# Key products 6 and 7 of the first parity in the opening, high copies ahead of low parts, and attention as a pipeline over units

## The chip, the cores and the metric

One core of a Trainium2 chip. The metric is the device time of one execution in microseconds, the median over several runs. Five engines work side by side, each from its own queue in order: TensorE (PE, matrix products), VectorE (DVE), ScalarE (ACT), GpSimd (POOL) and SyncE (SP). In this kernel POOL and SP mostly issue DMAs; a DMA that adds to what lies at its target (an accumulating DMA) is issued by POOL.

## The reference

The kernel mixes two branches of one input x (2048 tokens, 512 channels, fp32) by a gate per token. Branch a is local dilated attention (32 heads of 16, each token sees 8 tokens at distances 0, 2, ..., 14), branch b a gated feed-forward layer of width 1792:

```python
qkv = (x @ wqkv)                    # q, k, v for 32 heads of 16
idx = pos[:, None] - arange(8) * 2
logits = einsum("bhsd,bhswd->bhsw", q, k[idx]) * 16 ** -0.5    # masked where idx < 0
a = einsum("bhsw,bhswd->bhsd", softmax(logits), v[idx]) @ wo
b = (gelu(x @ w_gate) * (x @ w_up)) @ w_down
g = sigmoid((x * gate_w).sum(-1))
out = g * a + (1 - g) * b
```

## The kernel before

Tokens are handled in two parities (`par` 0 and 1, even and odd tokens), since the dilation of 2 never mixes them. Within a parity, tokens lie in 128 partitions of 8 each.

**Products in two halves.** Every fp32 operand is split in a high part (a copy rounded to fp32r) and a low part (the operand minus that copy), and a product is three matmuls: high by high, low by high, high by low. So each operand costs a ScalarE copy and one more step, in one of two ways: `split` (L82) copies on ScalarE and subtracts on VectorE; `split_by_dma` (L219) writes the negative on ScalarE, lets an accumulating DMA on POOL's queue add the operand, and copies the high part on ScalarE. Both forms stand all over the kernel: in `hidden` (L743) for the hidden activations, in `down_w` (L709) for the weights of the down product, in `operands` (L660) for gate and up.

**Seven products for eight.** Products of 2x2 blocks are made from seven block products with sums of operands (`s1` to `s4` of x, `t1` to `t4` of the weights), in the keys and queries (list `KEYS`, L450), the values (`values`, L335) and gate and up (`gate_up`). `sum_x` and `combine_b` make the sums on VectorE. `XOP` holds the split x operands, `QO` the split weights of the keys, `VO` those of the values.

**Stages.** An opening (from L1053) loads x and weights and does five of the seven key products of parity 0 by hand (`key_mm`, `third`), with part of the values. `values` then does the rest of the values and `ffn(0)` the feed-forward layer of parity 0 in 14 chunks of 128 hidden units (f = 0 to 13). In each chunk `gate_up` places seven gate and up products, with four `pieces` between them: in chunks f = 0 and 1 these are key products 6 and 7 (`key_one`, L467; indices 5 and 6 of `KEYS`), later they are down products (`down`) of the group of two chunks before. Then `keys` and `values` do parity 1's first products (the crossing between the parities), and `ffn(1)` its chunks. `key_one` also copies its bank to a tile `rt` on ScalarE (L473) and issues two accumulating DMAs on POOL's queue, into the stores of keys and queries in HBM (`store_b`, L462).

**Attention.** A generator `attention` (L589) runs over eight units (2 parities x 4 groups of 128 channels). For each unit `load_kq` loads keys and queries from the stores, `scores` multiplies and reduces on VectorE (L512, L515), `softmax` (L523) does maximum, subtraction, an exp on ScalarE, sum, reciprocal and scaling, and `mix` (L541) multiplies with the values and adds up (L552 to L560), then transposes and stores. All this is VectorE work but for the exp. `softmax` also issues a tiny exp on a tile `ahead` (L527), which brings the exp table into ScalarE ahead of the real exp (L531).

**What sets the order.** The program is written once in order, and a scheduler puts the instructions of each engine in a queue by priorities. Attention steps are drawn by `pull(budget)` between products: each yield of the generator names its cost, and `PACE` scales the budgets for parity 0 and 1. They get a priority 150 places behind their place (`BEHIND`). `paced` ties a step to the matmul before it, and `PIN` keeps the opening's VectorE steps in program order. The tiles rotate through few buffers (`BUFS`): `hh` and `hl` have six each and serve both as hidden activations and as stage tiles of the opening and the values (`stages`), `rt` has four. A generator `first` (L1166), drawn between the value products, makes the operands of chunk 0 and the sums t1 and b22 that key products 6 and 7 need.

## Time and profile before

| | |
|---|---|
| median of 3 runs | 606.97 us (605.94 to 610.77) |
| profiled execution | 604.98 us |
| its span, first to last instruction | 603.2 us |
| mean granted TensorE clock | 0.999 |
| instructions | 8342 |
| DMA | 144.07 MB, mean 239 GB/s |
| chain that ended last, share by engine | PE 42%, DVE 4%, DMA 3%, ACT 3% |

Busy times are shares of the span: an engine at 98% has 2% of idle time in all, and what it waited for in that time is what could be won. Each instruction's duration overlaps with its neighbour's, so a rate is read from starts, not from durations. A wait is named by the instruction that waited and the one that released it: "PE p L347 <- ACT s L354" is a matmul of line 347 into a bank p that stood until a ScalarE step of line 354 wrote or freed s.

### The profile page before, as it was taken

How to read it: one execution, taken by the hardware profiler on the slowest of the kernel's cores; microseconds unless marked ns; L12 is line 12 of the kernel's file. 1: busy time of each engine (PE TensorE's matmuls, PEld its weight loads, DVE VectorE, ACT ScalarE, POOL GpSimd, SP SyncE). 2: the span in 40 equal slices, each digit the busy share in tenths (PEclk: the TensorE clock that was granted, in tenths of full speed). 3: DMA queues.
4: the chain of work that ended last, by engine and by line, in shares of the span. 5: the costliest groups of instructions: out<-in, count | busy, mean ns of one | idle time of the engine just before them, and what ended most of it. 6: DMA issues, size and time to landing. Idle time of an engine off the chain costs nothing.

```text
span 603.2 us, 8342 instructions
## 1 busy us (share of the span) xinstructions
PE 589.9 (98%) x2743; PEld 488.5 (81%) x2743; DVE 529.5 (88%) x613; ACT 438.6 (73%) x777; POOL 131.2 (22%) x153
## 2 busy tenths in 40 slices
PE   9999999999999999999999999999999999999997
PEld 7779877788888887787889888888888888887885
DVE  6776998999899996999998998999799979896981
ACT  6669566678887769877877666667876877697732
POOL 0131572212121202112101382212121213131400
PEclk9999999999999999999999999999999999999999
DMA  8689999997898888899889999989979797976924
GB/s 305 204 237 293 274 275 284 245 271 203 237 254 217 246 242 225 228 265 322 262 257 310 271 287 271 273 209 250 283 166 265 179 277 173 277 163 203 124 68 156
DMA packets 98152, 144.07 MB, mean 239 GB/s; under 512 B 9023, under 2 KB 59327, under 8 KB 98110
## 3 DMA queue, kind: packets, MB, share of 16 engines
q1 hardware_dynamic: 74862, 105.08, 52.9%
q0 software_dynamic: 22960, 38.09, 35.8%
q8 instruction: 21, 0.34, 0.2%
q10 hardware_dynamic: 288, 0.39, 0.2%
q14 instruction: 21, 0.17, 0.1%
HBM read 69.83 MB, written 44.66 MB: 190 GB/s over the span
## 4 chain that ended last, share of the span: by engine, by line
PE 42%; DVE 4%; DMA 3%; ACT 3%; issue 1%; SPq 0%; POOL 0%; DVEq 0%; ACTq 0%
PE p L728 18%; PE p L775 6%; PE acc L775 6%; PE p L1000 5%; PE acc L459 2%; PE acc L1000 2%; DMA hl<-c 1%; PE acc L347 1%; PE p L347 1%; DMA g<-vwt 1%; DVE prod L512 1%; DVE S L87 1%; DVE g L234 1%; DVE raw L244 0%; DMA raw<-os 0%
## 5 line engine op out<-in xcount | busy, mean ns | idle before, releaser
L728 PE MATMUL p<-S,g 128*128 128x512 f32 x672 | 168.4, 389 | 0.6 <-ACT p L810 0.6
L728 PEld LDWEIGHTS p<-S,g 128*128 128x128 f32 x672 | 125.9, 188 | 27.0 <-ACT p L810 1.1
L728 PE MATMUL p<-A,g 128*128 128x512 f32 x504 | 126.6, 390 | 0.0
L728 PEld LDWEIGHTS p<-A,g 128*128 128x128 f32 x504 | 94.2, 188 | 20.2 <-DMA g<-raw 0.4
L512 DVE TENSOR_TENSOR prod<-kq 128x2048 f32<-128x2048 f32 x32 | 72.9, 2279 | 5.8 <-DMA kq<-kq 5.4
L552 DVE TENSOR_TENSOR prod<-v,lg 128x2048 f32<-128x2048 f32 x32 | 73.0, 2280 | 1.0
L515 DVE TENSOR_REDUCE lg<-prod 128x128 f32<-128x2048 f32 x32 | 73.0, 2280 | 0.1
L775 PE MATMUL p<-d,hh 128*128 128x512 f32 x224 | 69.0, 392 | 2.3 <-ACT p L769 1.6
L686 POOL DMA_DIRECT2D g<-raw x28 | 24.2, 866 | 180.2 <-ACT g L683 84.1
L775 PE MATMUL acc<-d,hh 128*128 128x512 f32 x224 | 59.6, 391 | 2.0 <-DMA d<-r 1.3
L739 ACT ACTIVATE c<-p 128x512 f32<-128x512 f32 x56 | 33.4, 597 | 31.7 <-PE p L728 24.0
L775 PEld LDWEIGHTS p<-d,hh 128*128 128x128 f32 x224 | 41.7, 188 | 12.7 <-ACT p L769 3.1
L775 PEld LDWEIGHTS acc<-d,hh 128*128 128x128 f32 x224 | 41.9, 188 | 11.7 <-DMA d<-r 1.7
L744 DVE TENSOR_TENSOR c<-c 128x512 f32<-128x512 f32 x56 | 37.9, 680 | 7.6 <-ACT c L841 7.5
L740 DVE TENSOR_TENSOR c<-c,s 128x512 f32<-128x512 f32 x56 | 38.0, 685 | 6.4 <-ACT c L739 6.4
L775 PE MATMUL p<-d,hl 128*128 128x512 f32 x112 | 42.6, 389 | 0.0
L733 ACT ACTIVATE s<-p 128x512 f32<-128x512 f32 x56 | 33.1, 592 | 10.6 <-PE p L728 10.0
L751 POOL DMA_DIRECT2D hl<-c x24 | 22.9, 971 | 75.6 <-ACT hl L750 49.6
L556 DVE TENSOR_TENSOR prod<-prod 128x1024 f32<-128x1024 f32 x32 | 39.0, 1220 | 0.4
L719 POOL DMA_DIRECT2D d<-r x23 | 19.7, 858 | 90.0 <-ACT d L718 47.1
L459 PE MATMUL acc<-d,S 128*128 128x512 f32 x144 | 35.7, 390 | 0.0
L775 PE MATMUL acc<-d,hl 128*128 128x512 f32 x112 | 35.2, 391 | 0.3 <-DVE hl L748 0.2
(209 smaller groups left out, 1076.4 us busy)
## 6 DMA issues: line engine op xcount, KB each, us to landing
g<-raw POOLq DMA_DIRECT2D x28, 512.0 KB, 6.3
raw<-wff SPq DMA_DIRECT2D x42, 256.0 KB, 4.6
ws<-g SPq DMA_DIRECT2D x14, 768.0 KB, 6.0
g<-ws SPq DMA_DIRECT2D x14, 768.0 KB, 6.8
r<-wff SPq DMA_DIRECT2D x28, 256.0 KB, 4.3
hl<-c POOLq DMA_DIRECT2D x24, 256.0 KB, 6.6
d<-r POOLq DMA_DIRECT2D x23, 256.0 KB, 6.9
v<-vs SPq DMA_DIRECT2D x8, 512.0 KB, 7.0
```

The lines of the kernel that those rows point to most:

```text
L459: LAST[:] = [nc.tensor.matmul(ps, x[:, ts], w, start=(start and kc == i == 0), stop=(kc == 1 and i == 2), skip_group_check=True)]
L512: paced(nc.vector.tensor_tensor(prod, spans(k, jj), q[:, jj:jj + 2, None, :].to_broadcast([P, 2, W, UC]), op=OP.mult))
L515: nc.vector.tensor_reduce(two_of(lg, jj), prod.rearrange("p j w (h d) -> p (j w) h d", d=DH), axis=AX.X, op=OP.add)
L552: paced(nc.vector.tensor_tensor(prod.rearrange("p j w (h d) -> p (j w) h d", d=DH), spans(v, jj).rearrange("p j w (h d) -> p j w h d", d=D ...
L556: nc.vector.tensor_tensor(prod[:, :, :4], prod[:, :, :4], prod[:, :, 4:], op=OP.add)
L728: LAST[:] = [nc.tensor.matmul(ps, w_, a_, start=(start and kc == 0 and n == 0), stop=(kc == 1 and n == 2), skip_group_check=True)]
L733: nc.scalar.activation(s, ps, AF.Copy)
L739: nc.scalar.activation(c, ps, AF.Copy)
L740: nc.vector.tensor_tensor(c, c, s, op=OP.add)
L744: nc.vector.tensor_tensor(ge, ge, up, op=OP.mult)
L775: LAST[:] = [nc.tensor.matmul(pp, a[:, ts], w, start=(i == 0 and n == 0 and gr == 0), stop=(i == 1 and n == 2), skip_group_check=True)]
L1000: LAST[:] = [nc.tensor.matmul(pa, a, b, start=(first and n == 0), stop=(last and n == 2), skip_group_check=True)]
```

## The change

- The opening takes key products 6 and 7 of parity 0: after `third(4)` it calls `key_one(0, k, t)` for k = 5 and 6 and all four t. Chunks f = 0 and 1 of `ffn(0)` have empty pieces. In parity 0 `key_one` writes its copies into stage tiles (`hh` and `hl` in turn) instead of `rt`. The sums t1 and b22 are made in the opening, no longer in `first`.
- In the opening the high copies are issued in one go on ScalarE (`late_split`, `late_s`, `late_b`), and the low parts wait in a list `low` from which `lows(n)` issues n at a time on VectorE.
- `hidden` uses the form with the VectorE subtract for all chunks; before, chunks with even f above 0 used the accumulating DMA. `down_w` uses it for f < 3 in both parities (before: f < 2 and f < 3).
- Attention: `softmax` is cut into `exps` (up to the exp) and `shares` (from the sum), and the `ahead` step is dropped. Scores and exps of the next unit come before the mix of this one, its shares after. Values are loaded ahead of that (`load_values`), and the keys of the unit after next ahead of the mix.
- `PACE` goes from (1.05, 1.22) to (1.1, 1.25).

```diff
-PACE = (1.05, 1.22)
+PACE = (1.1, 1.25)
...
-        st = tl("rt")
+        st = tl("rt" if par else next(stages))[:, :512]
...
-    def softmax(par, u):
+    def exps(par, u):
         lg = LG[par, u]
         m = pool.tile([P, UH, NP], F32, name="m")
         nc.vector.tensor_reduce(m, lg, axis=AX.X, op=OP.max)
-        nc.scalar.activation(pool.tile([P, 32], F32, name="ahead")[:W, :1], m[:W, 0, :1], AF.Exp, scale=0.0)
         yield 0.7
         nc.vector.tensor_tensor(lg, lg, m[:, :, :, None].to_broadcast([P, UH, NP, W]), op=OP.subtract)
         yield 0.7
         nc.scalar.activation(lg, lg, AF.Exp, scale=DH ** -0.5)
+
+    def shares(par, u):
+        lg = LG[par, u]
+        m = pool.tile([P, UH, NP], F32, name="m")
         nc.vector.tensor_reduce(m, lg, axis=AX.X, op=OP.add)
...
+        def logits(i, wait):
+            if units[i] not in LG:
+                load_kq(*units[i])
+                if wait:
+                    yield LOAD
+            yield from scores(*units[i])
+            yield from exps(*units[i])
+            ready.append(i)
...
         for i, un in enumerate(units):
-            if scored == i:
+            if i not in ready:
                 yield from need(un[0], un[1] // 2 * 2)
-                load_kq(*un)
-                yield LOAD
-                yield from scores(*un)
-                scored += 1
-                mixed = False
-            yield from need(un[0], 1)
-            yield from softmax(*un)
...
+                yield from logits(i, i > 0)
+            if i not in shared:
+                yield from share(i)
+            load_values(*un)
+            if keyed(i + 1):
+                yield from logits(i + 1, False)
+                if keyed(i + 2):
+                    load_kq(*units[i + 2])
+            yield from mix(*un)
             done.add((*un, "o"))
...
+            if i + 1 in ready:
+                yield from share(i + 1)
...
     def down_w(par, f):
...
-        if f < 2 + par:
+        if f < 3:
...
     def hidden(key, ge, up):
...
-        if key[0] % 2 or not key[0]:
-            nc.scalar.activation(hh_, ge, AF.Copy)
-            nc.vector.tensor_tensor(hl_, ge, hh_.bitcast(F32), op=OP.subtract)
-        else:
-            nc.scalar.activation(hl_, ge, AF.Copy, scale=-1.0)
-            nc.gpsimd.dma_start(hl_.bitcast(F32), ge, accum_op=OP.add)
-            nc.scalar.activation(hh_, ge, AF.Copy)
+        nc.scalar.activation(hh_, ge, AF.Copy)
+        nc.vector.tensor_tensor(hl_, ge, hh_.bitcast(F32), op=OP.subtract)
...
-                pieces = [[lambda t=t: key_one(par, 5 + f, t)] for t in range(BT)]
+                pieces = [[lambda t=t: key_one(par, 5 + f, t)] if par else [] for t in range(BT)]
...
+    def late_split(name, kc, x):
+        hi, lo, raw = x
+        nc.scalar.activation(hi, raw, AF.Copy)
+        low.append((lo, raw, hi))
+
+    def lows(n):
+        for _ in range(n):
+            lo, raw, hi = low.pop(0)
+            paced(nc.vector.tensor_tensor(lo, raw, hi.bitcast(F32), op=OP.subtract))
...
     third(2)
     room_b("t4")
+    lows(1)
     for kc in range(2):
         combine_b("t4", "b21", "b21", "t2", kc)
-        split_b("t4", kc)
-        split_x(0, 1, 2 + kc)
+        late_b("t4", kc)
+        lows(1)
...
+    room_b("t1")
+    for kc in range(2):
+        combine_b("t1", "b11", "b22", "t2", kc)
+        late_b("t1", kc)
+        lows(2)
     third(3)
+    lows(len(low))
+    room_b("b22")
+    for kc in range(2):
+        late_b("b22", kc)
...
     third(4)
     PIN[0] = False
     done.add((0, 0))
     PACING[0] = True
+    for k in 5, 6:
+        for t in range(BT):
+            key_one(0, k, t)
+            next(made, None)
...
         combine(1)
         fetch_d(0)
-        yield
-        for n in "t1", "b22":
-            room_b(n)
-            for kc in range(2):
-                if n == "t1":
-                    combine_b("t1", "b11", "b22", "t2", kc)
-                split_b(n, kc)
-                yield
```

More of the change, by code (lines that the diff above doesn't have):

```diff
@@ L539, in softmax, with load_values, mix @@
         yield 0.7
-    def mix(par, u, pause):
-        lg = LG.pop((par, u))
+    VT = {}
+    def load_values(par, u):
         hh, c = divmod(u, 2)
-        v = pool.tile([P, 2 * NP - 1, UC], F32, name="v")
+        VT[par, u] = v = pool.tile([P, 2 * NP - 1, UC], F32, name="v")
         load_slots(v, VS[par, hh][c])
-        yield pause
+    def mix(par, u):
+        lg, v = LG.pop((par, u)), VT.pop((par, u))
         tb = pool.tile([P, 2, BT * UC], F32, name="tb")
@@ L590, in attention, with keyed, share @@
         units = [(0, u) for u in range(NU)] + [(1, u) for u in range(NU)]
-        yield from need(0, 0)
-        load_kq(0, 0)
-        yield from scores(0, 0)
-        yield from need(0, 1)
-        scored, mixed = 1, False
+        ready, shared = [], []
+        def keyed(i):
+            return i < len(units) and (units[i][0], units[i][1] // 2 * 2) in done
+        def logits(i, wait):
[6 more added lines that the diff above has]
+            ready.append(i)
+        def share(i):
+            yield from need(units[i][0], 1)
+            yield from shares(*units[i])
+            shared.append(i)
         for i, un in enumerate(units):
-            if scored == i:
+            if i not in ready:
                 yield from need(un[0], un[1] // 2 * 2)
-                load_kq(*un)
-                yield LOAD
-                yield from scores(*un)
-                scored += 1
-                mixed = False
-            yield from need(un[0], 1)
-            yield from softmax(*un)
-            to = units[scored] if scored < len(units) else None
-            ahead = to and (to[0], to[1] // 2 * 2) in done
-            if ahead:
-                load_kq(*to)
-            yield from mix(*un, LOAD if mixed else 0.0)
+                yield from logits(i, i > 0)
[7 more added lines that the diff above has]
+            yield from mix(*un)
             done.add((*un, "o"))
-            mixed = not ahead
-            if ahead:
-                yield from scores(*to)
-                scored += 1
+            if i + 1 in ready:
+                yield from share(i + 1)
     fill = attention()
@@ L1101, in tile_gated_mix, with late_s, late_b @@
               for kc in range(2))
+    low = []
+    def late_split(name, kc, x):
[6 more added lines that the diff above has]
+            paced(nc.vector.tensor_tensor(lo, raw, hi.bitcast(F32), op=OP.subtract))
+    def late_s(n, kc):
+        i = {"s1": 3, "s2": 0, "s4": 1, "s3": 2}[n]
+        raw = S1.pop(kc) if n == "s1" else XR[kc][:, i * 512:(i + 1) * 512]
+        XOP[n, kc] = pair("S")
+        late_split(n, kc, (*XOP[n, kc], raw))
+    def late_b(n, kc):
+        late_split(n, kc, (*QO[n, kc], QR[n, kc]))
     for kc in range(2):
@@ L1104, in tile_gated_mix @@
             sum_x(kc, n)
+        late_s("s2", kc)
         if not kc:
@@ L1109, in tile_gated_mix @@
                 next(made)
-        split_s("s2", kc)
+        else:
+            lows(1)
         combine_b("t3", "b12", "b22", "b12", kc)
         combine_b("t2", "b11", "t3", "b11", kc, OP.add)
-        split_b("t2", kc)
-        if not kc:
-            for t in range(2, BT):
-                take_first(Z_[t], t, first_copy[t % 2])
+        late_b("t2", kc)
+        if kc:
+            lows(2)
+    room_b("t3")
+    for kc in range(2):
+        late_s("s3", kc)
+        late_b("t3", kc)
+        lows(1)
+    for t in range(2, BT):
+        take_first(Z_[t], t, first_copy[t % 2])
     values(0, iter(()), lambda k: None, range(2))
@@ L1122, in tile_gated_mix @@
     PACING[0] = False
-    room_b("t3")
-    for kc in range(2):
-        split_s("s3", kc)
-        split_b("t3", kc)
     def third(k, after=iter(())):
@@ L1143, in tile_gated_mix @@
     room_b("t4")
+    lows(1)
     for kc in range(2):
         combine_b("t4", "b21", "b21", "t2", kc)
-        split_b("t4", kc)
-        split_x(0, 1, 2 + kc)
+        late_b("t4", kc)
+        lows(1)
+    for kc in range(2):
+        late_split("a22", kc, (*X[0, 1, 2 + kc], XR[kc][:, 1536:]))
+        sum_x(kc, "s4")
+        late_s("s4", kc)
     set_x(0)
+    lows(2)
     for kc in range(2):
-        sum_x(kc, "s4")
-        split_s("s1", kc)
-        split_s("s4", kc)
-    third(3)
+        late_s("s1", kc)
+    room_b("t1")
+    for kc in range(2):
+        combine_b("t1", "b11", "b22", "t2", kc)
+        late_b("t1", kc)
+        lows(2)
+    third(3)
+    lows(len(low))
+    room_b("b22")
+    for kc in range(2):
+        late_b("b22", kc)
+    for f in range(2):
+        fetch(f)
     room_v(*LARGE)
@@ L1156, in tile_gated_mix @@
     next(made)
-    for f in range(2):
-        fetch(f)
+    lows(len(low))
     next(made)
@@ L1176, in first @@
         fetch_d(0)
-        yield
-        for n in "t1", "b22":
-            room_b(n)
-            for kc in range(2):
-                if n == "t1":
-                    combine_b("t1", "b11", "b22", "t2", kc)
-                split_b(n, kc)
-                yield
     def step(k):
```

## The prediction

> **What bounds the kernel now.** I read the page's busy times first, then a table of busy time by stage, then what TensorE waited for, then single stretches of the timeline. On the page:

> ```profile
> PE 589.9 (98%) x2743; PEld 488.5 (81%) x2743; DVE 529.5 (88%) x613; ACT 438.6 (73%) x777; POOL 131.2 (22%) x153
> ```

> TensorE is busy for all but 13.3 of the span's 603.2 us. The change neither adds nor drops a matmul (2743 in both instruction orders), so it can win back only a part of those 13.3 us; what it can lose has no such limit. Where they lie is told by the table of stages (length, PE, PEld, DVE, ACT and POOL busy, clock, DMA share, GB/s):

> ```profile
> 0.00:42.00 42.00, 38.75 (x199) 31.26 (x199) 28.92 (x51) 28.30 (x60) 9.70 (x22) 1.00 0.76 246
> 42.00:60.00 18.00, 17.83 (x133) 17.16 (x134) 12.32 (x23) 15.94 (x40) 1.77 (x2) 1.00 0.99 289
> 60.00:84.00 24.00, 24.00 (x107) 19.86 (x107) 23.55 (x24) 12.84 (x27) 14.76 (x12) 1.00 1.15 267
> 84.00:116.00 32.00, 29.18 (x124) 22.55 (x123) 29.75 (x40) 24.37 (x40) 10.45 (x11) 1.00 1.08 281
> 116.00:232.00 116.00, 116.00 (x513) 96.08 (x512) 108.55 (x123) 89.55 (x148) 18.61 (x22) 1.00 0.88 235
> 232.00:246.00 14.00, 12.44 (x52) 9.33 (x52) 10.57 (x11) 13.90 (x22) 2.60 (x3) 1.00 0.86 214
> 246.00:272.00 26.00, 26.00 (x116) 21.52 (x116) 25.90 (x33) 19.96 (x35) 4.28 (x5) 1.00 0.95 264
> 272.00:284.00 12.00, 11.18 (x48) 8.32 (x47) 12.00 (x10) 8.59 (x16) 2.16 (x3) 1.00 1.06 326
> ...
> 520.00:585.00 65.00, 64.69 (x285) 52.99 (x284) 57.53 (x62) 46.99 (x81) 14.61 (x17) 1.00 0.71 155
> 585.00:603.20 18.20, 14.09 (x63) 11.33 (x61) 3.40 (x6) 3.62 (x6) 0.00 (x0) 0.98 0.41 144
> ```

> PE loses 3.25 us in the opening, 2.82 in the first feed-forward chunks (84 to 116), 1.56 at 232 to 246, 0.82 at 272 to 284, 0.31 near the end of the second parity and 4.1 in the tail. The third column shows the other thing to watch: VectorE has 210.3 us of work in the 224 us from 60 to 284, and from 246 to 284 it is full. The waits of PE say who was late:

> ```profile
> PE p L775 <- ACT p L769: 1.6, 3, 0.8
> PE acc L775 <- DMA d<-r: 1.3, 1, 1.3
> PE p L347 <- ACT s L354: 1.3, 1, 1.3
> ...
> PE p L347 <- ACT g L86: 1.0, 1, 1.0
> ...
> PE acc L775 <- ACT rt L473: 0.7, 1, 0.7
> PE p L728 <- ACT p L810: 0.6, 1, 0.6
> ```

> **The opening.** ScalarE's high copies now come ahead of all low parts, and VectorE's subtractions are queued behind them. The two waits of the opening, 1.3 on s (L354) and 1.0 on g (L86), are for ScalarE copies that stood behind a split's turn. I take both as gone: -2.3 us, with bounds of -3.25 (all idle of 0 to 42) and +1.0 (one such wait more). What comes in: 48 matmuls of key products 6 and 7. Their rate is in the timeline of PE, where six take 1.36 us from start to start:

> ```profile
> 105.78 1.52 PE L728 MATMUL p<-A,g 128*128 128x512 f32 x6
> 107.14 0.39 PE L775 MATMUL acc<-d,hl 128*128 128x512 f32 x1
> ...
> 110.43 1.88 PE L775 MATMUL acc<-d,hh 128*128 128x512 f32 x7 [1.31 <-DMA d<-r]
> ```

> So 48 x 0.227 = 10.9 us of PE time moves from the chunks f = 0 and 1 (5.4 each) to the opening: no change in the sum. With them go eight ScalarE copies and, for the sums t1 and b22, six VectorE steps of 0.68 (4.1 us). Both fit: the stage 42 to 60 leaves VectorE 5.7 us idle and becomes 10.9 us longer. Without that room the 4.1 would be late for the first feed-forward chunk.

> The products' 16 accumulating stores move with them on POOL's queue, ahead of the accumulating load of chunk 0's operand g1:

> ```profile
> ks<-rt POOLq DMA_DIRECT2D x8, 128.0 KB, 9.2
> qs<-rt POOLq DMA_DIRECT2D x8, 128.0 KB, 10.1
> ```

> They read the stage tiles hh and hl (before: rt), which the value products want back 10 to 15 us later; with a landing of 9 to 10 us that is just in time. If they landed later, ScalarE would stop at the copy into the tile and all its later copies with it. I take nothing here, and put the price of a late landing into the next part.

> **Chunks f = 0 to 2.** Gone: the wait on rt L473 (0.7), since no key bank is emptied there, and the wait on d<-r (1.3, the row at 110.43), since with f < 3 the chunk's low part comes from a VectorE subtract instead of an accumulating DMA. That is -2.0. On the other side, chunks 0 and 1 have 5.4 us less of PE work each over unchanged ScalarE and VectorE work, and VectorE has 23.55 of 24 us busy at 60 to 84. Nothing before shows a chunk so short; the bounds are 0 and one chunk's lost cover, 5.4 us. Most of the work has its operands made in the longer opening, so I take a value near the lower end, that of a wait which stands there now: +0.8.

> **The hidden halves.** In 24 of 56 halves a ScalarE copy and an accumulating DMA give way to a VectorE subtract:

> ```profile
> L748 DVE TENSOR_TENSOR hl<-c,hh 128x512 fp32r<-128x512 f32 x32 | 21.7, 681 | 4.3 <-ACT hh L747 4.3
> L750 ACT ACTIVATE hl<-c 128x512 fp32r<-128x512 f32 x24 | 15.1, 628 | 4.9 <-DVE c L744 4.9
> L751 POOL DMA_DIRECT2D hl<-c x24 | 22.9, 971 | 75.6 <-ACT hl L750 49.6 <-ACT c L739 10.8 <-DMA os<-tb 9.5
> L512 DVE TENSOR_TENSOR prod<-kq 128x2048 f32<-128x2048 f32 x32 | 72.9, 2279 | 5.8 <-DMA kq<-kq 5.4
> ```

> ScalarE loses 15.1 us and POOL 22.9; VectorE gains 24 x 0.68 = 16.3 (8.2 in each parity). Over the whole kernel that is 546 of 603 us, still under PE. It does no harm where VectorE has slack, and the second parity has it (57.53 of 65 at 520 to 585, so the 0.3 lost there goes too). The first parity is another matter, below.

> **232 to 246.** ScalarE is full there (13.90 of 14), because it swaps tables four times around one `ahead` preload:

> ```profile
> 230.04 1.28 ACT L527 ACT_TABLE_LOAD   x1
> 231.34 0.20 ACT L527 ACTIVATE ahead<-m 8x1 f32<-8x1 f32 x1
> 231.56 1.28 ACT L841 ACT_TABLE_LOAD   x1
> 232.85 0.60 ACT L841 ACTIVATE c<-p 128x512 f32<-128x512 f32 x1
> 233.96 1.28 ACT L531 ACT_TABLE_LOAD   x1
> ...
> 240.63 1.28 ACT L825 ACT_TABLE_LOAD   x1
> ```

> A gelu came between the preload and its exp, so the exp table was loaded twice. Without the preload two loads are left, which frees 2.6 us, and the hidden halves free 0.6 each. I take the waits there as gone, -1.5 of the 1.56. The exp itself now stands behind its own load, but the new order puts a whole mix between exp and its use, so nobody waits. [...]

> **The crossing to the second parity, 272 to 300.** VectorE must split the second parity's sums there. In the changed kernel's order, between the last gelu product of the first parity (it waits for a PE result) and the low part of s2, the first that PE reads across the crossing from a sum, VectorE has 37 steps: 28 of the 128x512 kind, two mix products, two halvings, five small ones. Their spacing:

> ```profile
> 260.18 2.28 DVE L552 TENSOR_TENSOR prod<-v,lg 128x2048 f32<-128x2048 f32 x1
> 262.50 1.23 DVE L556 TENSOR_TENSOR prod<-prod 128x1024 f32<-128x1024 f32 x1
> 263.64 0.68 DVE L744 TENSOR_TENSOR c<-c 128x512 f32<-128x512 f32 x1
> 264.24 0.68 DVE L558 TENSOR_TENSOR prod<-prod 128x512 f32<-128x512 f32 x1
> 264.96 0.42 DVE L560 TENSOR_TENSOR o<-prod 128x256 f32<-128x256 f32 x1
> ```

> 28 x 0.60 + 2 x 2.28 + 2 x 1.2 + 5 x 0.4 = 25.8 us. PE has 85 matmuls between the same points, 85 x 0.227 = 19.3, and the activation that hands the result over takes 0.6 to 0.9. So PE stops for 25.8 + 0.8 - 19.3 = 7.3; I take +7.2. In the order before, about 10 us less of attention stands in that stretch, and the same count gives about 1, as 0.82 was seen. Bounds: +9 if VectorE comes late to the stretch, and 0 if what is queued there overlaps more than these starts show. The old 0.8 goes.

> **The sum.** -2.3 - 2.0 + 0.8 - 1.5 - 0.3 - 0.8 + 7.2 = +1.1 us; the tail keeps its 4.1. The profiled execution took 604.98 us, 1.8 beyond its span; it becomes 606.1. It lies 2.0 under the median of 606.97, with three runs spread over 4.8; on the median's footing it would be 608.1. I predict halfway, 607.0. Its own range is 602 to 612.

> **Rivals.** Faster: the stall at the crossing doesn't come, and the rest of the sum holds: -6.1, or 598.9 to 600.9, say 600; without the 0.8 of chunks 0 and 1, 599. For it: each removed wait stands by name in the list, and at 272 to 284 a full VectorE cost PE only 0.8. Against it: 25.8 us in a room of 19.3. It decides if PE's stall near 290 is under 1.5. Chance 0.2.

> Slower: VectorE bounds the first parity. It has 210.3 us of work from 60 to 284, and gains 8.2 + 0.7 - 4.1 = 4.8, while PE's time there shrinks by 10.9 to 213.1. If VectorE also keeps its 13.7 idle us (waits for ScalarE and DMA), it needs 228.8, 15.7 too much; a start 3.5 earlier (of the 5.4 it waited for kq, L512) leaves 12. The 4.3 of stalls in that stretch (2.0 + 1.5 + 0.8) are swallowed, the opening gives 2.3, and VectorE comes late into the crossing (9 there instead of 7.2, 1.8 more): 12 - 4.3 - 2.3 + 1.8 = +7.2, which is 612.2 by the profiled execution and 614.2 by the median, 613 halfway. It decides once VectorE has no gap before each gelu product from about 120 on. Against it: attention can slide into the second parity. [...] Chance 0.25.

> Late start: the 16 stores in the opening meet DMA engines that are full (share 0.99 at 42 to 60), land late and hold ScalarE: 5.4 instead of 0.8 in chunk 0, +5.7, so 611 to 613. Chance 0.1, half of it beyond 1%.

> The forecast keeps 0.45. One per cent, 6.1 us, is about what can be told from no change here. The faster rival lies beyond it; the slower one stands just beyond 613, and I count 0.2 of its 0.25, with 0.05 of the late start. So 0.2, 0.55, 0.25. The range goes to 599 for the faster rival and 615 for the slower.

> **What would show it.** The PE waits on s L354, g L86, rt L473, d<-r and at 232 to 246 should be gone; ACT_TABLE_LOADs before exp should be single; a PE wait of 5 to 9 us on a VectorE low part (L87, tile S) should stand near 290, with VectorE gapless before it. No such wait, or many waits on hl (L760) at 120 to 260, would make the sum wrong.

## The result, and the profile after

The changed kernel takes 626.98 us in the median (625.34 to 630.68, 4 runs), the kernel before 606.58 (605.94 to 610.77, 4 runs): a ratio of 1.033, with a 95% interval of 1.026 to 1.040. It is slower by some 20 us; I had forecast 607, at most 615. (Further down, the one run of e3_cross and the one of the kernel before that lie over 1.5% above the fastest of their kernel are left out.) The profiled execution took 628.07 us, with a span of 626.3. Its page begins:

```profile
PE 596.8 (95%) x2743; PEld 495.6 (79%) x2743; DVE 539.0 (86%) x638; ACT 423.8 (68%) x743; POOL 109.8 (18%) x128
```

The edits did to the amounts what they say: VectorE gained 9.5 us (the durations of its instructions add up to 17.0 more, as forecast; the page counts time in which two of them overlap once), ScalarE lost 14.8, POOL 21.4, and PE has as many matmuls as before. But PE is idle for 29.5 us instead of 13.3, and it waits for other things than before (PE's waits: us in all, times, longest):

```profile
PE p L783 <- DVE hl L760: 6.6, 1, 6.6
PE acc L459 <- ACT S L128: 6.2, 1, 6.2
PE acc L347 <- DVE c L87: 3.5, 1, 3.5
PE p L741 <- DVE g L692: 2.4, 1, 2.4
PE p L1008 <- DMA S<-raw: 1.7, 1, 1.7
PE p L741 <- ACT c L752: 1.2, 1, 1.2
PE acc L347 <- DMA g<-vwt: 1.1, 1, 1.1
```

None of the waits quoted of before is left, and few long ones have come. To place them I use PE's lateness: the end of a matmul, less the time that all matmuls up to it need at PE's rate at a granted clock of 1.00 (0.2267 us for 512 columns and 0.1183 for 258, whose median spacing in both traces is 0.227 and 0.119; for the 31 warm ones of 128 columns 0.06, an estimate, 128/512 of the 0.2267, where the traces show a spacing of 0.107; 581.1 us in all). It counts a stall and the slow matmuls behind it alike. Worked out from the matmul records of both profiled executions, by stretches of PE's own work, it grows by (us). The wait on d<-r, which the forecast has among the chunks 0 to 2, stands at 98.8 us of work, so its 1.3 is forecast here for the stretch from 98 on:

| PE work done | stretch | before | after | difference | forecast |
|---|---|---|---|---|---|
| 0 to 57 | opening | 7.9 | 5.8 | -2.1 | -2.3 |
| 57 to 98 | end of the values, chunks 0 to 2 | 2.7 | 11.3 | +8.6 | +0.1 |
| 98 to 262 | rest of the first parity | 4.2 | 0.1 | -4.1 | -2.8 |
| 262 to 300 | crossing | 1.5 | 11.6 | +10.1 | +6.4 |
| 300 to 350 | values of the second parity | 0.6 | 1.7 | +1.1 | 0 |
| 350 to 372 | chunk 1 of the second parity | 0.0 | 8.8 | +8.8 | 0 |
| 372 to 581 | rest and tail | 1.2 | 2.1 | +0.9 | -0.3 |

The differences add up to 23.3 us, the difference of the two profiled executions (628.07 - 604.98 = 23.1) but for the tail behind the last matmul. Three stretches lose 27.5 us.

**Chunks 0 to 2.** VectorE's timeline (start, us, engine, instruction, idle time before it and its releaser), with the matmul that waits:

```profile
50.59 0.70 DVE L167 TENSOR_TENSOR v<-v,tb 128x516 f32<-128x516 f32 x1 [0.20 <-PE acc L459]
63.96 2.29 DVE L512 TENSOR_TENSOR prod<-kq 128x2048 f32<-128x2048 f32 x1 [12.67 <-DMA kq<-kq]
66.16 0.69 DVE L87 TENSOR_TENSOR c<-v,c 128x516 fp32r<-128x516 f32 x1
```
```profile
66.91 0.83 PE L347 MATMUL acc<-c,A 128*128 128x258 f32 x4 [3.54 <-DVE c L87]
```

VectorE stands idle for 12.67 us (before: 5.4) for a load that only attention needs. Behind it in VectorE's queue is the low part c, 0.7 us of work whose operands have long been there; PE needs it and stops for 3.54 us. ScalarE stands too, for 4.78 us, until an accumulating store of the key products has read a stage tile:

```profile
65.48 0.38 ACT L354 ACTIVATE hh<-acc 128x256 f32<-128x256 f32 x1 [4.78 <-DMA qs<-hh]
```

From 63.96 to 90 VectorE then has no gap, and in chunk 0 PE waits twice more, for a low part that stands behind score products on VectorE and for a ScalarE step:

```profile
82.64 1.20 PE L741 MATMUL p<-A,g 128*128 128x512 f32 x4 [2.39 <-DVE g L692]
85.05 2.92 PE L741 MATMUL p<-S,g 128*128 128x512 f32 x6 [1.21 <-ACT c L752]
```

The three waits are 7.1 of the 11.3 us; the rest is mostly matmuls that run slowly behind them (the granted clock is 0.57 from 67 to 70, 0.75 from 83 to 86 and 0.76 from 86 to 90).

**Chunk 1 of the second parity.** The same picture: the first score product of a unit whose loads were issued at 378 to 381, ahead of the low part of a hidden half.

```profile
394.30 2.29 DVE L512 TENSOR_TENSOR prod<-kq 128x2048 f32<-128x2048 f32 x1 [8.85 <-DMA kq<-qs]
396.51 0.69 DVE L528 TENSOR_TENSOR lg<-lg,m 128x512 f32<-128x512 f32 x1
397.11 0.68 DVE L760 TENSOR_TENSOR hl<-c,hh 128x512 fp32r<-128x512 f32 x1
```
```profile
397.85 1.22 PE L783 MATMUL p<-d,hl 128*128 128x512 f32 x2 [6.62 <-DVE hl L760]
```

**The crossing.** This stall was forecast. VectorE has no gap from 286 to 308; PE stops for 6.16 us, for the high copy of S on ScalarE, which had itself waited 3.64 us for VectorE's sum, and for 0.81 us for the low part on VectorE. Then it runs slowly, as the clock column (the third from the end) of the stages shows:

```profile
300.00:304.00 4.00, 0.00 (x0) 0.00 (x0) 4.00 (x5) 0.46 (x1) 0.00 (x0) 0.87 0.95 278
304.00:308.00 4.00, 2.97 (x6) 1.96 (x7) 4.00 (x7) 1.84 (x4) 0.00 (x0) 0.50 0.28 80
308.00:312.00 4.00, 4.00 (x11) 3.03 (x11) 1.88 (x4) 0.00 (x0) 0.00 (x0) 0.50 0.00 0
312.00:316.00 4.00, 4.00 (x17) 3.22 (x16) 2.58 (x4) 2.58 (x6) 0.00 (x0) 0.85 0.23 66
```

From 308 to 312 PE is busy all the time, with 11 matmuls where 4 us hold 17 or 18 at the rate of before. The granted clock is 0.50.

### The profile page after: what moved, and what is told of

Read it like the earlier page. It is cut to its first block, busy times and chain, and to the rows that moved or that the text cites. A ratio compares the mean times of both kernels' runs of the same rounds, so it can differ in the third digit from the quotient of the medians.

```text
span 626.3 us, 8255 instructions
## 1 busy us (share of the span) xinstructions
PE 596.8 (95%) x2743; PEld 495.6 (79%) x2743; DVE 539.0 (86%) x638; ACT 423.8 (68%) x743; POOL 109.8 (18%) x128
## 3 DMA queue, kind: packets, MB, share of 16 engines
q0 software_dynamic: 19360, 31.53, 28.7%
## 4 chain that ended last, share of the span: by engine, by line
PE 62%; DMA 15%; issue 10%; DVE 5%; ACT 4%; POOL 2%; SPq 1%; POOLq 0%; DVEq 0%; ACTq 0%
PE p L741 31%; PE p L783 9%; PE acc L783 9%; PE p L1008 5%; PE acc L459 3%; DMA kq<-qs 2%; DMA qs<-hh 2%; PE acc L1008 2%; PE p L347 2%; DMA S<-raw 1%; DMA g<-raw 1%; DMA raw<-wff 1%; DMA vs<-hl 1%; PE p L459 1%; DMA raw<-xt 1%
## 5 line engine op out<-in xcount | busy, mean ns | idle before, releaser
L512 DVE TENSOR_TENSOR prod<-kq 128x2048 f32<-128x2048 f32 x32 | 73.0, 2281 | 21.7 <-DMA kq<-kq 12.7
L558 DVE TENSOR_TENSOR prod<-v,lg 128x2048 f32<-128x2048 f32 x32 | 72.7, 2272 | 4.2 <-DMA v<-vs 3.5
L699 POOL DMA_DIRECT2D g<-raw x28 | 26.1, 932 | 259.8 <-ACT g L696 175.3
L783 PEld LDWEIGHTS acc<-d,hh 128*128 128x128 f32 x224 | 42.5, 190 | 9.0
L783 PE MATMUL p<-d,hl 128*128 128x512 f32 x112 | 42.5, 397 | 6.6 <-DVE hl L760 6.6
L759 ACT ACTIVATE hh<-c 128x512 fp32r<-128x512 f32 x56 | 35.0, 626 | 11.3 <-DVE c L757 11.3
L760 DVE TENSOR_TENSOR hl<-c,hh 128x512 fp32r<-128x512 f32 x56 | 38.2, 684 | 2.7 <-ACT hh L759 2.6
```

Source lines behind the costliest of these rows:

```text
L512: paced(nc.vector.tensor_tensor(prod, spans(k, jj), q[:, jj:jj + 2, None, :].to_broadcast([P, 2, W, UC]), op=OP.mult))
L558: paced(nc.vector.tensor_tensor(prod.rearrange("p j w (h d) -> p (j w) h d", d=DH), spans(v, jj).rearrange("p j w (h d) -> p j w h d", d=D ...
L759: nc.scalar.activation(hh_, ge, AF.Copy)
L760: nc.vector.tensor_tensor(hl_, ge, hh_.bitcast(F32), op=OP.subtract)
L783: LAST[:] = [nc.tensor.matmul(pp, a[:, ts], w, start=(i == 0 and n == 0 and gr == 0), stop=(i == 1 and n == 2), skip_group_check=True)]
```

## Experiments

Each time below is a median, each ratio is to the kernel before, run on the same chip. The growth of PE's lateness by stretch is worked out as above from each kernel's one profiled execution (opening, chunks 0 to 2, rest of the first parity, crossing, second parity up to 350, to 372, to 575, end):

| kernel | open | 57-98 | 98-262 | cross | -350 | -372 | -575 | end |
|---|---|---|---|---|---|---|---|---|
| before | 7.9 | 2.7 | 4.2 | 1.5 | 0.6 | 0.0 | 1.2 | 0.0 |
| after | 5.8 | 11.3 | 0.1 | 11.6 | 1.7 | 8.8 | 2.1 | 0.0 |
| e1_pause | 5.1 | 12.3 | 0.1 | 10.6 | 4.0 | 0.0 | 0.0 | 16.3 |
| e2_first | 5.8 | 11.1 | 3.5 | 6.0 | 4.6 | 0.0 | 1.2 | 7.8 |
| e3_cross | 8.3 | 13.4 | 0.1 | 0.3 | 10.1 | 1.0 | 2.9 | 3.2 |
| e5_all | 5.1 | 10.5 | 3.3 | 0.0 | 0.3 | 0.1 | 0.0 | 17.1 |
| o_open | 5.1 | 9.8 | 3.5 | 2.3 | 3.8 | 0.0 | 0.4 | 0.0 |
| o_att | 8.0 | 7.3 | 5.8 | 8.5 | 0.3 | 2.0 | 4.5 | 0.0 |
| o_hid | 8.0 | 7.6 | 0.1 | 11.6 | 0.6 | 0.0 | 0.5 | 0.0 |
| x_att | 5.3 | 9.5 | 0.1 | 6.7 | 0.2 | 0.0 | 0.3 | 4.9 |
| o_nostore | 6.8 | 5.6 | 4.6 | 2.3 | 4.2 | 0.0 | 0.7 | 0.0 |
| o_late | 5.4 | 7.7 | 1.4 | 2.9 | 0.6 | 0.2 | 0.7 | 0.0 |
| late_h_cross | 5.6 | 4.7 | 2.4 | 4.3 | 0.2 | 0.0 | 0.5 | 5.4 |
| e7_pace | 6.4 | 7.2 | 2.5 | 0.0 | 0.3 | 0.0 | 0.0 | 14.0 |
| e8_fewer | 6.0 | 10.2 | 4.8 | 6.7 | 1.5 | 0.0 | 0.1 | 16.6 |
| e9_both | 5.2 | 10.5 | 3.2 | 5.8 | 1.9 | 0.0 | 0.1 | 11.0 |

### Each stall mended by itself, and all three together

e1_pause, scores put off behind their load; the pause of the second parity's first unit grows with it:

```diff
                 if wait:
-                    yield LOAD
+                    yield 12.0
...
-                yield from logits(i + 1, False)
+                yield from logits(i + 1, units[i + 1][0])
```

> Only in the second parity, the scores of a unit whose keys have just been asked for are put off by 12 us of credit. Theory (head of the line): VectorE's first score product of the second unit of that parity waited 8.8 us for its load, with the low part of a hidden half behind it, and TensorE lost 6.6 us at 391 and ran at a granted clock near 0.5 for about 4 us behind it, 9 us in all. They go: 617 to 619 us. Rival (VectorE is short of time as a whole because of the 24 added subtracts): the work is only moved, another wait on VectorE takes the place of this one, 624 to 628.

635.19 us, 1.045 (1.038 to 1.052), slower still. The stall at 391 is gone, as the theory says (8.8 to 0.0), but 16.3 us come up at the end, where PE waits for the attention of the last unit. That is the rival's outcome, and more than it gave. In o_att below, with the same order of attention, VectorE waits 4.67 us for that unit's load and PE loses 2.0 in the stretch; in e2_first and e3_cross, with the same order too, the wait is under 1 us. So the missing pause lets this stall come in some orders and not in others; that this depends on how the load lies in time is a guess, since I did not vary it by itself.

e2_first, the first unit's scores put off:

```diff
+            if not i:
+                yield 12.0
             yield from scores(*units[i])
```

> The first unit's scores are put off by 12 us of credit; in the order the low part c of the values then stands ahead of the first score product instead of behind it. Theory (head of the line): the wait on c L87 at 63 (3.5 us) and its slow clock go, and of the waits at 80 to 90 at least half: 5 to 8 us. The order at the crossing moves too, to 20.0 us of VectorE work in a room of 18.6, which counts to a stall of 2.2 in place of 7.2, too short for a slow clock of long: 5 to 9 us more. Sum 610 to 617. Rival (the two chunks without key products are too short for their VectorE work): the wait at 80 to 90 stays or grows by what the first one loses, and only the crossing gains: 618 to 622.

623.45 us, 1.026 (1.018 to 1.033). The low part c is in time now, but chunks 0 to 2 lose as much as they did: PE's longest wait there is for a ScalarE copy.

```profile
PE acc L347 <- ACT hh L354: 4.0, 1, 4.0
```

Line 354 copies a value product into a stage tile hh, which has to wait until the accumulating store of key products 6 and 7 has read it. So the stores hold PE in two ways, and where one is mended it waits on the other. The time is near the rival's, but its longest wait is not the one that the rival named. At the crossing the count (a stall of 2.2) agrees: the waits on S are 1.8 and 0.4, and the stretch lost 6.0 instead of 11.6. That a stall so short brings no slow clock for long was my estimate: the stretch lost 3.8 more than these waits, and in clockgap below a gap of 1.90 cost 1.6. The loss in chunk 1 is gone too (8.8 to 0.0), but 7.8 come up at the end.

e3_cross, no attention drawn around the crossing:

```diff
-            pull(n * PACE[par] * (1.0 if par or f + 1 < FC else 0.8))
+            pull(n * PACE[par] * (1.0 if par or f + 2 < FC else 0.0))
...
-                pull((0.2, 0.2, 0.6, 1.2, 1.2)[k])
+                pull((0.0, 0.0, 0.6, 1.2, 1.2)[k])
```

> No attention is drawn in the last two chunks of the first parity and the first two key products of the second. Theory (a stretch too full): VectorE has 14.7 us of work in a room of 19.3 at the crossing, so the wait on the high and low parts of S near 298 (6.2 and 0.8) goes with the clock of 0.5 behind it, 9 to 11 us: 616 to 619. Rival (VectorE bounds the first parity, or is short as a whole): the attention left out there comes back as a wait in the second parity or at the end, 624 to 628.

621.28 us, 1.024 (1.016 to 1.032). The crossing loses 0.3 instead of 11.6: the count of VectorE's work against PE's room is right. But 10.1 come up behind it in the second parity and 3.2 at the end, as the rival says. The time lies between the theory's and the rival's: one profiled execution each, and 6 us of the 11 reach the median.

e5_all, the three edits in one:

> The three edits together. Theory (three separate places in VectorE's order): 9 + 6 + 10 us go and nothing comes in their place, about 602, between 599 and 606, which would be at or under the kernel before. Rival (VectorE is short as a whole): attention ends later by the pauses and the tail waits for it, 612 to 622.

622.34 us, 1.024 (1.019 to 1.030). Up to the end PE is as late as in the kernel before (19.2 against 18.0 us). The crossing and chunk 1 are mended. The first place is not: chunks 0 to 2 still lose 10.5, with a wait of 3.3 on the copy of line 354 as in e2_first, and what makes up for it is the opening and other stretches that lose less than before. Then 17.1 us go at the very end, on two waits:

```profile
599.12 3.65 PE L1010 MATMUL acc<-S,hh 128*128 128x512 f32 x8 [4.24 <-ACT hh L86]
612.95 1.22 PE L1010 MATMUL p<-S,hh 128*128 128x512 f32 x2 [9.27 <-ACT hh L86]
```

The tile hh holds attention's last result, and VectorE works on that until 606, with nothing else to do:

```profile
591.89 0.71 DVE L571 STREAM_TRANSPOSE tb<-o 128x512 f32<-128x512 f32 x1
592.53 2.25 DVE L558 TENSOR_TENSOR prod<-v,lg 128x2048 f32<-128x2048 f32 x1
594.81 1.23 DVE L562 TENSOR_TENSOR prod<-prod 128x1024 f32<-128x1024 f32 x1
...
605.64 0.71 DVE L571 STREAM_TRANSPOSE tb<-o 128x512 f32<-128x512 f32 x1
```

### The parts of the change, one at a time

Three kernels take the kernel before and one part each; x_att takes the changed kernel with the attention and pace of before (the first and third parts together). The edits are those of the diff above: o_open has the opening with the moved key products, o_att `exps`, `shares`, `load_values`, the new `attention` and `PACE`, o_hid `hidden` and `down_w`.

> Only the first part of the change on top of the kernel before: the opening with key products 6 and 7 and the late low parts. Theory (head of the line): VectorE's first score product still stands ahead of the low part c, and its load still meets the accumulating stores, so the stall of some 5 us at 63 to 70 and some of the waits at 80 to 90 are there; no crossing stall (13.7 us of VectorE work in a room of 19.3) and none at 391. Against the kernel before +4 to +8: 610 to 615. Rival (the added subtracts are the cost): at or under the kernel before, 602 to 607.

615.55 us, 1.011 (1.007 to 1.016), 8.0 over the kernel before: at the upper end of the theory's range, with the waits on c L87 (2.2) and g L679 (2.3) at the places named. Not expected were 3.2 us more than before in the values of the second parity, where PE waits 2.2 for the load of a weight part c.

> Only the second part on top of the kernel before: attention as a pipeline, with the new pace. Theory: the stall on the load of the keys at 391 (9 us), because scores follow their load without a pause, and at the crossing 21.1 us of VectorE work in a room of 18.6, 3.4 us of stall and 1 to 2 of slow clock. The waits at 232 to 246 go (-2). Against the kernel before +10 to +14: 617 to 621. Rival (the pipeline is harmless and only VectorE's added work or the opening costs): 603 to 609.

623.24 us, 1.025 (1.020 to 1.030), 15.6 over. The size is near the theory's, but much of it at other places, so the size is in part luck. Chunk 1 of the second parity loses only 2.0. The crossing loses 8.5, but the wait on S that was counted at 3.4 is only 0.35: PE stands 3.36 us just before it for a ScalarE copy (L433), which in ScalarE's queue is behind a step that waits 4.86 us for PE's last down products. And 7.3 are lost in chunks 0 to 2, where PE waits 4.3 us for an accumulating DMA into a gate operand:

```profile
PE p L741 <- DMA g<-raw: 4.7, 2, 4.3
```

> Only the third part on top of the kernel before: every hidden half and the down weights of chunk 2 by a VectorE subtract. Theory: 16.9 us more on VectorE and nothing moved otherwise; at the crossing 23.3 us of work in a room of 18.6, a stall of 5.6 and 2 to 4 of slow clock; nothing at 391. Against the kernel before +6 to +9: 612 to 616. Rival (VectorE is short as a whole): also waits on low parts of hidden halves all along and a later end of attention, +14 or more, over 620. Rival (VectorE has room): within 2 us of the kernel before.

610.52 us (10 runs), 1.0048 (1.0022 to 1.0073), 2.9 over, between the theory and the rival with room. The profiled execution is this kernel's slowest, 615.03, so its stretches show more loss than the median does. The waits from 98 to 262 are gone (4.2 to 0.1): this part gives the gain there. At the crossing the wait on S was 4.5 us where the count gave 5.6, after another of 3.36 on the copy of L433. In chunks 0 to 2 PE waits 3.8 us for the same kind of accumulating DMA as in o_att.

> The changed kernel with the attention and the pace of the kernel before. Theory: the stall at 391 goes (9), the crossing has 17.7 us of work in a room of 18.6 and loses at most 1 instead of 11; the stalls at 63 to 90 stay. 626.98 - 19 = 608, between 606 and 613. Rival (VectorE short as a whole): 618 or more, with the loss at the end of the kernel.

614.57 us, 1.011 (1.007 to 1.015). The size misses the theory by 2 and is under the rival. The count of at most 1 at the crossing holds for the waits on S (none), but the stretch loses 6.7, by the copy of L433 (3.35) and slow matmuls behind it; 4.9 are lost at the end. Without the new attention the kernel is 12 us faster than the changed one. The parts don't add: singly 8.0, 15.6 and 2.9, in all 26.5, together 20.4. In the traces the overlap is at the crossing, where the second and third parts lose 8.5 and 11.6 singly and 11.6 together; it is not the same wait in each.

### Why the first keys come late

o_nostore is o_open with the first parity's stores of key products 6 and 7 left out:

```diff
-        store_b(nc.gpsimd, par, st, BT + t if k == 5 else t, 1, accum_op=OP.add)
+        if par:
+            store_b(nc.gpsimd, par, st, BT + t if k == 5 else t, 1, accum_op=OP.add)
```

> The first part alone, with the 16 accumulating stores of key products 6 and 7 of the first parity left out (the keys and queries of half of that parity's channels are incomplete). VectorE's order in the opening is the same, the first score product still ahead of the low part c. Theory (the stores crowd the DMA engines and the load of the first keys lands late): the wait of VectorE on that load falls from 11.3 to 5 to 7 us, the wait on c L87 (2.2) goes, and the loss of the stage from PE's 57th to 98th us of work falls from 9.8 to 4 to 6; 615.6 - 5 = 609 to 612. Rival (the chunks without key products are too short): wait on the load shorter, stage still 8 or more, 613 to 616. Rival (the load is late whatever the stores do): VectorE's wait stays at 10 to 12.

610.77 us, 1.004 (1.001 to 1.007), 4.8 under o_open. VectorE's wait for the load, in o_open and in o_nostore:

```profile
DVE prod L512 <- DMA kq<-kq: 11.3, 1, 11.3
```
```profile
DVE prod L513 <- DMA kq<-kq: 3.9, 1, 3.9
```

The load itself lands 3.7 us after its issue in o_nostore, in o_open 6.1 and 8.4 for its two parts (7.3 and 9.2 in the changed kernel). ScalarE's wait for a stage tile (5.26 in o_open) and PE's wait on c are gone, and the stretch from 57 to 98 loses 5.6 instead of 9.8. So the stores in the opening are what makes the first keys late and holds ScalarE, and the order makes PE pay for it. What stays is two waits in chunk 0, on VectorE's low part g (1.41) and on a ScalarE step (1.90), and 2.3 that no wait names, which I take for slow matmuls behind them (the run's mean granted clock is 0.997): there the chunk without key products is too short for its VectorE work, since VectorE has no gap from its first score product to 82.

### The slow clock by itself

clockgap runs blocks of 100 matmuls and lets TensorE wait for a VectorE chain of growing length between them.

> Measures the slow clock by itself: blocks of 100 fp32r matmuls of 512 columns (22.7 us at six per 1.36 us), between which TensorE waits for a VectorE chain of growing length, 0.7 to 8 us. It computes nothing of the reference. Theory: after a gap of 2 to 3 us and more the granted clock falls to 0.5 for the next 4 to 8 us and that block is 1.5 to 4.5 us longer, after shorter gaps it isn't. Rival (the slow matmuls behind the stalls come from waits that the trace doesn't name): every block takes the same time whatever the gap ahead of it.

The ten blocks, with the gap ahead of each in brackets; the first, with no block ahead of it, took 24.85:

```profile
4.29 24.85 PE L41 MATMUL p<-mov,w 128*128 128x512 f32 x100 [4.29 <-ACT w L31]
29.78 22.98 PE L41 MATMUL p<-mov,w 128*128 128x512 f32 x100 [0.64 <-DVE w L47]
54.13 22.97 PE L41 MATMUL p<-mov,w 128*128 128x512 f32 x100 [1.37 <-DVE w L47]
79.00 24.57 PE L41 MATMUL p<-mov,w 128*128 128x512 f32 x100 [1.90 <-DVE w L47]
106.21 24.60 PE L41 MATMUL p<-mov,w 128*128 128x512 f32 x100 [2.63 <-DVE w L47]
133.78 24.59 PE L41 MATMUL p<-mov,w 128*128 128x512 f32 x100 [2.97 <-DVE w L47]
162.07 24.52 PE L41 MATMUL p<-mov,w 128*128 128x512 f32 x100 [3.70 <-DVE w L47]
190.83 25.45 PE L41 MATMUL p<-mov,w 128*128 128x512 f32 x100 [4.23 <-DVE w L47]
221.57 25.44 PE L41 MATMUL p<-mov,w 128*128 128x512 f32 x100 [5.30 <-DVE w L47]
254.64 24.32 PE L41 MATMUL p<-mov,w 128*128 128x512 f32 x100 [7.63 <-DVE w L47]
```

After 0.64 and 1.37 us a block takes 22.98; after 1.90 to 3.70 it takes 1.5 to 1.6 more, after 4.23 and 5.30 2.5 more, after 7.63 1.3 more. That it takes a gap of 2 to 3 us was my estimate; the gap of 1.90 had its price too. The price does not grow steadily with the gap, and the records of the granted clock, which every trace holds, show why. In them the clock is 1.00 or 0.50, and the slow time comes in steps of 3.41 us on a fixed grid: in clockgap it begins at 80.05, 107.36, 134.66, 161.97, 189.28, 220.00 and 250.72, always 8 or 9 steps apart, and in the changed kernel at 67.42, 84.49, 302.94 and 395.10, which are 5, 64 and 27 steps apart, and lasts 1, 1, 3 and 2 steps. Here is the grid's step that holds the gap of 1.90, the two behind it, and last the step that holds the gap of 1.37 (length, PE busy; the clock is the third column from the end):

```profile
76.64:80.05 3.41, 1.51 (x8) 0.92 (x7) 1.74 (x3) 0.00 (x0) 0.00 (x0) 1.00 0.00 0
80.05:83.46 3.41, 3.41 (x10) 2.67 (x9) 0.00 (x0) 0.00 (x0) 0.00 (x0) 0.50 0.00 0
83.46:86.88 3.42, 3.42 (x17) 2.81 (x16) 0.00 (x0) 0.00 (x0) 0.00 (x0) 1.00 0.00 0
52.74:56.15 3.41, 2.04 (x10) 1.67 (x10) 1.21 (x3) 0.00 (x0) 0.00 (x0) 1.00 0.02 5
```

I laid this grid over the traces of all kernels here that have slow time before their end (the kernel before has none). A step at full clock in which PE was idle for 0.56 of the time or more was followed by a slow one in 49 of 49 cases, with 0.46 or less in none of 2586; between 0.47 and 0.55 both occur. A slow step was followed by another one whenever PE was idle for 0.18 of it or more (30 cases), and never with 0.16 or less (53). So what counted in these traces is how a gap lay on the grid, and how much work fell into the slow steps. At the crossing of two kernels PE has the same gap before the same 24 matmuls. In x_att (first line) the slow clock follows; in late_h_cross (second line), where the gap lies half in one step and half in the next (0.46 and 0.52 idle), it doesn't:

```profile
293.95 8.34 PE L459 MATMUL p<-d,A 128*128 128x512 f32 x24 [3.35 <-ACT p L433]
291.26 5.76 PE L459 MATMUL p<-d,A 128*128 128x512 f32 x24 [3.36 <-ACT p L433]
```

In the changed kernel's crossing three steps are slow (302.94 to 313.18), and PE's lateness grows from 17.5 to 28.7: 6.97 in the two waits, 4.3 in slow matmuls.

### Taking what wins

o_late keeps of the change only the order of the opening, and leaves key products 6 and 7 in the chunks:

```diff
-        split_b("t2", kc)
-        if not kc:
-            for t in range(2, BT):
-                take_first(Z_[t], t, first_copy[t % 2])
+        late_b("t2", kc)
+        if kc:
+            lows(2)
...
-        split_b("t4", kc)
-        split_x(0, 1, 2 + kc)
-    set_x(0)
+        late_b("t4", kc)
+        lows(1)
```

> Only the order of the opening (high copies first, low parts behind) on top of the kernel before; key products 6 and 7 stay in chunks 0 and 1, and so do the sums t1 and b22 in the generator between the values. Theory: the two named waits of the opening (2.3 us) go and nothing else changes: 604 to 605.5 against 607.6. Rival (the gain of the opening is lost again because the first keys' load and not TensorE sets when attention starts): 606.5 to 608.

606.32 us (12 runs) against 607.72, 0.9964 (0.9939 to 0.9988): faster than the kernel before by 0.4%, just under the rival's range and above the theory's. The opening gains 2.5 us in the trace, more than that is lost again in the chunks behind it (2.7 to 7.7) and at the crossing (1.5 to 2.9), and 2.8 come back from 98 to 262. In all, the one profiled execution is no less late than that of the kernel before (18.8 against 18.0), so the trace doesn't place the median's gain.

late_h_cross takes this opening, the third part, and less attention at the crossing:

```diff
-PACE = (1.05, 1.22)
+PACE = (1.05, 1.27)
...
-            pull(n * PACE[par] * (1.0 if par or f + 1 < FC else 0.8))
+            pull(n * PACE[par] * (1.0 if par or f + 1 < FC else 0.0))
...
-                pull((0.2, 0.2, 0.6, 1.2, 1.2)[k])
+                pull((0.0, 0.0, 0.6, 1.2, 1.2)[k])
```

> The opening's order as in the run before this one, every hidden half by the VectorE subtract and chunk 2's down weights too, the attention of the kernel before, but no attention drawn in the last chunk of the first parity nor in the first two key products of the second, and a pace of 1.27 in the second parity to catch up. Theory: the opening gives 2.5, the waits from 116 to 262 (4 us) go, the crossing has 18.3 us of VectorE work in a room of 18.6 and loses about 1: 600 to 604, ahead of the kernel before. Rival (VectorE is short as a whole): 17 us more VectorE work end later than the tail's need, 606 to 612.

612.94 us, 1.009 (1.006 to 1.012): near the rival's upper end. The crossing loses 4.3 where about 1 was counted; the waits on S are 0.37, and PE stands 3.36 for the copy of L433. The profiled execution, the fastest of the twelve, is at 17.7 us of lateness before the end, as good as the kernel before, and loses 5.4 there.

### What makes the end late

Three kernels on top of e5_all: e7_pace sets `PACE = (1.1, 1.4)`, e8_fewer takes the old `hidden`, e9_both does both.

> The three repairs, with a pace of 1.4 instead of 1.25 in the second parity. If the pace alone makes the end late: attention is drawn 12 per cent faster, some 20 us sooner by the end, the 17 us at the end fall under 5 and the time to 606 to 611. If VectorE's amount of work does: it has 4 to 5 per cent idle in the second parity, some 12 us, so the end comes less than 12 us earlier and low parts of hidden halves begin to hold TensorE on the way: 613 to 622.

> The three repairs, with the hidden halves of the kernel before (24 by the accumulating DMA), the pace of the change. If the amount of VectorE's work makes the end late: 16.3 us less of it, 8 of them in the second parity, bring the end 8 to 16 us earlier: 606 to 614. If the pace does: attention is drawn at the same places, so the end stays, 17 us lost: 619 to 624.

> The three repairs, the hidden halves of the kernel before, and the pace of 1.4 in the second parity. Either cause is mended, so the end loses under 4 us: 603 to 609. If it stays over 612, the end is late for a third reason, and both readings fall.

618.55 us, 1.019 (1.013 to 1.025); 632.61, 1.040 (1.035 to 1.045); 623.72, 1.024 (1.018 to 1.031). Neither is the cause by itself, and with both the end still loses 11.0: both readings fall, as the last expectation has it. More than that, e8_fewer is 10 us slower than e5_all. From the records of VectorE I then took, for each kernel, the start of its first score product, its busy and idle time from there to the end of the last transposition, and PE's lateness before the end (at 575 us of work):

| kernel | first product | busy | idle | last transposition | lateness | difference | lost at the end |
|---|---|---|---|---|---|---|---|
| before | 60.5 | 484.9 | 39.7 | 585.1 | 18.0 | 567.1 | 0.0 |
| o_late | 61.1 | 482.3 | 42.5 | 585.8 | 18.8 | 567.0 | 0.0 |
| after | 64.0 | 493.6 | 40.9 | 598.5 | 41.3 | 557.2 | 0.0 |
| o_att | 60.4 | 478.7 | 47.3 | 586.3 | 36.5 | 549.8 | 0.0 |
| o_open | 61.9 | 486.5 | 45.8 | 594.2 | 25.0 | 569.1 | 0.0 |
| o_nostore | 56.3 | 486.6 | 50.6 | 593.5 | 24.3 | 569.2 | 0.0 |
| o_hid | 61.1 | 499.3 | 39.0 | 599.3 | 28.3 | 571.0 | 0.0 |
| x_att | 62.2 | 499.6 | 34.3 | 596.0 | 22.1 | 573.9 | 4.9 |
| late_h_cross | 58.4 | 496.2 | 36.9 | 591.6 | 17.7 | 573.9 | 5.4 |
| e3_cross | 67.7 | 496.4 | 46.2 | 610.3 | 36.2 | 574.1 | 3.2 |
| e2_first | 63.8 | 494.9 | 50.1 | 608.8 | 32.3 | 576.5 | 7.8 |
| e9_both | 62.2 | 482.4 | 62.0 | 606.6 | 26.7 | 579.8 | 11.0 |
| e7_pace | 66.8 | 496.7 | 36.7 | 600.3 | 16.3 | 584.0 | 14.0 |
| e1_pause | 62.7 | 499.5 | 55.5 | 617.7 | 32.0 | 585.7 | 16.3 |
| e8_fewer | 63.2 | 485.3 | 66.9 | 615.5 | 29.2 | 586.3 | 16.6 |
| e5_all | 62.1 | 497.3 | 47.0 | 606.4 | 19.2 | 587.1 | 17.1 |

The last transposition is the sum of the three columns before it. What is lost at the end goes with the difference between it and PE's lateness: nothing up to 569 (in o_hid up to 571), and above that about what it exceeds 569 to 571 by (late_h_cross 573.9 and 5.4, e5_all 587.1 and 17.1). So the end is a race between two chains, PE's with its stalls and VectorE's from its first score product on, and in the kernel before VectorE is only 2 to 4 us ahead of the point where it sets the time. In e9_both VectorE has no more work than before but 22.3 us more idle time. From 270 to 370 it is idle for 27 us, against 5 before and 16 in e5_all, and its longest waits there are on ScalarE (5.2) and PE (4.8); the work taken from it came back as idle time, and why is not shown further. In e7_pace the idle time is no more than before, but the work is 11.8 us more and the first score product starts 6.4 later. So more idle time in one kernel, and more work with a later start in the other, make the end late.

## Why the prediction was wrong

**The opening, -2.3.** Right: -2.1 in the changed kernel, and the two named waits are gone.

**"I take nothing here", on the 16 stores moved into the opening.** This step failed. In the changed kernel the load of the first keys lands after 7.3 and 9.2 us (before: 3.7 and 6.5), and VectorE stands for 12.67 us. With the stores the wait is 11.3 (o_open), without them 3.9 (o_nostore). The prediction had the DMA share of 0.99 and the landing of 9 to 10 us, and asked only who waits for the stores' tiles. It named the late start as a rival at a tenth, with ScalarE held; that rival's path is real (ScalarE stands 4.78 us in the changed kernel, and PE 4.0 for it in e2_first), but in the changed kernel PE waits on another that I had not asked for: what is queued on VectorE behind the first score product.

**Chunks 0 to 2, -2.0 + 0.8.** The two waits did go. The cover of the lost key matmuls was sized at 0.8, and this term was too small; the stretch lost 8.6 more than before, of which the stores account for 4.2 in o_open (9.8 against 5.6). Without the stores two waits of 1.41 and 1.90, in all 3.3, stay in chunk 0, the place of the 0.8, and 2.3 that no wait names. o_att, o_hid and o_late lose there too, on an accumulating DMA into a gate operand, and why that comes late is open.

**98 to 262, -1.5, and -1.3 for d<-r.** Right, with a size too small: -4.1. The waits named are gone; the rest are waits under 0.2 us each, on which the forecast put nothing. For 232 to 246 I had two reasons, the dropped preload and the hidden halves. In o_att, with the first alone, the longest wait left there is 0.4, and in o_hid, with the second alone, none over 0.2 is left.

**The crossing, +7.2 - 0.8.** Right in mechanism and place: 25.8 us in a room of 19.3 gave waits of 6.97 us on the high and low parts of S from 298 on. That the longest of them ended with a ScalarE copy and not, as I had it, with VectorE's low part changes little, since that copy waited for VectorE's sum. The same count over other orders gave 2.2, 0, 0, 5.6 and 3.4, where the waits on S were 2.2, none, 1.6, 4.5 and 0.35 (e2_first, e3_cross, o_open, o_hid, o_att), so that it comes so near here is in part luck. Missing was the price of the slow clock behind it, 4.3 us. Nothing in the trace of before could show it: its longest stall was 1.31 us, and its clock never fell in a stretch that I quoted but the last.

**The second parity, 0.** This step failed. I had costed the new order of attention by what it adds to VectorE's work, and not by the loads: of the unit whose keys were not there yet, the scores now follow their load without the pause of before. VectorE waited 8.85 us for it, and 8.8 us of time were lost: a wait of 6.62 on a low part and slow matmuls behind it, mended by a pause (e1_pause).

**The rivals.** The faster one fell: the stall came. "VectorE bounds the first parity" fell as it was put: from 98 to 262 the lateness grows by 0.1 only. But VectorE is short in another way, over its whole chain. That hidden cost of the added subtracts doesn't show in the changed kernel, whose PE is late enough to leave VectorE time; it shows in each repair.

**Range.** The four misses, 3.7 at the crossing, 8.8 in chunk 1, 8.5 in chunks 0 to 2 and -1.3 from 98 to 262, are 19.7 of the 22.2 us between the forecast (+1.1) and the difference in the table (+23.3).

## What to carry to other kernels

Before an instruction is put in an engine's queue behind which others stand, ask what it waits for, and what a move does to that. Here VectorE's first score product waited 12.67 us for its load, the low part c queued behind it was late, and PE stood for 3.54; and the stores that were moved into the opening made the load late (VectorE waits 11.3 us with them in o_open, 3.9 without them in o_nostore). Count, stretch by stretch, the work between two points of one engine's order against the other engine's work between the same points; here this found the place of the longest stall before it was run and its size to 0.3 us, while over five other orders it was off by 0 to 3 us, the most where another wait came just ahead. And where a second engine's chain is nearly as long as the first's, look at both before a stall is mended on the first: VectorE's chain had only 2 to 4 us to spare in the kernel before, and with the three edits of e5_all 17.1 us were lost at the end.
